# P times V in tiles of 64 rows by 32 columns, each half of a key tile in a PSUM bank of its own

## The chip, the core and the metric

The kernel runs on one core of a Trainium2 chip. The metric is device time of one execution, in microseconds. Three runs of the kernel before took 1716.6 to 1716.94 us, with a median of 1716.67 us.

A core has five engines that run on their own and wait for one another through semaphores. TensorE (PE in the profile) multiplies matrices and writes the products to PSUM, which has eight banks of 128 partitions by 512 float32 values. ScalarE (ACT) and VectorE (DVE) read PSUM, GpSimd (POOL) does not. SyncE (SP) issues nearly all DMAs here.

## The reference

A transformer block with adaptive layer norm, on x of 2048 rows by 512 columns, in float32:

```python
mod = (silu(c) @ w_mod).reshape(1, 6, 1, 512)        # sa, ca, ga, sb, cb, gb
h = layernorm(x) * (1 + ca) + sa
q = (h @ wq) as 32 heads of 16;  k = h @ wk;  v = h @ wv     # one k and one v for all heads
p = softmax(q @ k.T * 16 ** -0.5)
x = x + ga * ((p @ v, heads side by side) @ wo)
h = layernorm(x) * (1 + cb) + sb
x = x + gb * (((h @ w_gate) * (h @ w_up)) @ w_down)          # 512 -> 1792 -> 512
```

The change is in `p @ v`: for each head, 2048 queries by 2048 keys, times 2048 keys by 16 values.

## The kernel before

**Attention.** The 2048 query rows are cut into NB = 4 blocks of 512 and the 32 heads into 8 groups of four: 32 units `u`, each a block of queries and four heads. A unit walks over KT = 16 key tiles of 128 keys; one such step is here called a step, and there are 512 of them. In a step:

- `qk_exp` (line 627) makes, for each of four heads, the scores with keys on partitions and queries on columns (tile `sc`, line 631), and ACT writes their exponential to SBUF as the float32 tile `P` (line 633). Letter e in the order of the step.
- `max_half` and `max_mm` (lines 1050 and 576) make, for the next unit, scores with queries on partitions (tile `mx`, line 581); DVE reduces each to its maximum over 512 keys (line 584). Letter m. The maxima are subtracted inside a later score product, so that the exponential is that of a softmax.
- `pv` (line 637) multiplies V's tile by the four `P` tiles of the key tile one step back. V's tile `vst` has 32 columns: 16 values, and ones that give the sum of the exponentials. Head j's result goes to partitions 32j to 32j + 31 of one PSUM tile, `pvb[u]`, in which all 16 key tiles are summed.

Scores and maxima are float16 products with 48 or 50 rows, split over the two halves of PE's rows by the index `a`: two of them, on different halves, run at the same time. P times V is in float32 and uses all 128 rows and 32 columns for each head.

**Side work.** Between those, PE works on the projections and the gated feed-forward part of the block (tile `side`, line 499; letter x). A group of such products sums in one bank. It too is split into row halves: while a step's e and m use one half, its x use the other, and `half` (line 506) adds a wait for an exponential when the half changes.

**Order.** `attend` (line 1142) writes the order of a pair of steps out by hand. In the early units (projections of q as side work) it is `FEW`, later `MANY`; in `MANY` a step has four e, four m and eight x in the order e m e e m m m e. At the end of a step come the evictions of ended side groups (`finish`) and then `pv` of the step before. A unit's last `pv` therefore runs in the next unit's first step, and `pv_out` of the ended unit is kept in `ends`, which is run in the middle of the step after that:

```python
                if j == len(order) // 2:
                    for f in ends:
                        f()
```

`pv_out` (line 645) copies `pvb[u]` to SBUF (`ev`, ACT, line 648), scaled per partition by `evs`, and five DMAs carry `ev` on to `oc` and `rs`, which `normalise` reads later.

**Banks.** The eight banks are a queue, `pool`. `ps_hold` takes the oldest entry and keeps it until `ps_give` puts it back at the end; `ps_mx`, which `sc` and `mx` use, takes the oldest and puts it back at once, so that its next user waits for whoever still reads it:

```python
        tag, bufs = pool.popleft()
        ...
        pool.append((tag, bufs))
```

`pvb[u]` is held for a whole unit, the side group for its length. A new side group may begin in a step in which the one before it ended; that one's bank comes back at the end of the step.

After the 32 units follow, with nothing of attention beside it, the rest of the side work and the feed-forward part of the last block of queries.

Of the kernel before, what the change touches and what calls it, by code (L numbers as in the profile page):

```python
# [15 lines left out]
AF = mybir.ActivationFunctionType  # L16
OP = mybir.AluOpType
# [8 lines left out]
KT = S // 128  # L26
# [27 lines left out]
def adaln_mqa_glu_kernel(ctx: ExitStack, tc: tile.TileContext, x_in, wq_in, wk_in, wv_in, wo_in,  # L54
                         wg_in, wu_in, wd_in, c_in, wm_in, out):
    nc = tc.nc
# [13 lines left out]
    def ps_hold(name="side", shape=(128, 512)):  # L70

        tag, bufs = pool.popleft()
        t = psum.tile(list(shape), F32, name=name, tag=tag, bufs=bufs)
        held[id(t)] = (t, tag, bufs)
        return t

    def ps_give(t):
        _, tag, bufs = held.pop(id(t))
        pool.append((tag, bufs))
# [53 lines left out]
    vst = consts.tile([128, KT, 32], F32, name="vst")  # L133
    nc.gpsimd.memset(vst, 1.0)
    sst = []
    for i in range(3):
        t = consts.tile([128, 2, BT], F16, name=f"sst{i}")
# [152 lines left out]
    for k in range(KC):  # L290
        for j in range(4):
            nc.tensor.matmul(pmA[32 * j:32 * j + 32, 0:256], silr[:, k, 0:32], wmA[:, k, 256 * j:256 * j + 256],  # L292
                             start=(k == 0), stop=(k == KC - 1))
# [77 lines left out]
    evs = consts.tile([128, 1], F32, name="evs")  # L371
# [249 lines left out]
    pvb = {}  # L621
    ptl = {}
# [13 lines left out]

    def pv(u, kt):
        if kt == 0:
            pvb[u] = ps_hold("pv")
        for j in range(4):  # L640
            p, a = divmod(j, 2)
            nc.tensor.matmul(pvb[u][32 * j:32 * j + 32, :], vst[:, kt, :], ptl[u, kt, p, a],  # L642
                             start=(kt == 0), stop=(kt == KT - 1))

    def pv_out(u):
        b, g = divmod(u, UB)
        ev = work.tile([128, BT], F32, name="ev", tag="ev", bufs=3)
        nc.scalar.activation(ev, pvb[u], AF.Copy, scale=evs)
        ps_give(pvb[u])
        if g % 2 == 0:  # L650
            oc[b, g // 2] = work.tile([128, BT], F32, name="oc", tag="oc", bufs=2)
            rsum[b, g // 2] = dram.tile([8, BT], F32, name=f"rs{b}_{g // 2}")
        h = 4 * (g % 2)
        for j in range(4):
            r = 16 * (h + j)
            nc.sync.dma_start(oc[b, g // 2][r:r + 16, :], ev[32 * j:32 * j + 16, :])
        nc.sync.dma_start(rsum[b, g // 2][h:h + 4, :], ev[16:128:32, :])
# [484 lines left out]
    def attend(u, kt):  # L1142
# [9 lines left out]
        for turn in range(2):  # L1152
# [23 lines left out]
            if v >= 0:  # L1176
                pv(*divmod(v, KT))
                if v % KT == KT - 1:
                    ends.append(lambda: pv_out(u - 1))
# [37 lines left out]
    u = NU - 1  # L1217

    pv(u, KT - 1)
    pv_out(u)  # L1220
    if cur:
        for r in range(2):
# [55 lines left out]
```

## Time and profile before

| what | value |
|---|---|
| median of three runs | 1716.67 us (1716.6 to 1716.94) |
| span of the profiled execution, first to last instruction | 1713.5 us |
| PE busy | 1666.1 us, 97% |
| DVE busy | 1393.1 us, 81% |
| ACT busy | 1218.4 us, 71% |
| POOL busy | 505.1 us, 29% |
| mean granted clock of PE | 0.993 |
| first and last eviction of a unit (start of `ev`) | 140.0 and 1539.5 us |

The page gives no time of the profiled execution beside its span; the runs are some 3 us longer than the span. In the rows of the trace, PE is a matmul and PEld its weight load; a matmul in float32 appears as two records with a weight load each. A row of the timeline has the start in us from the start of the span, the duration, engine, line, operation, the tile written and those read, rows times columns of the array (128*32), the operand's shape and a count if several follow one another. A group of the page has, behind the count, the busy time in us and the mean in ns, and then the idle time of the engine ahead of it and what ended it. A stretch has the busy time of PE, PEld, DVE, ACT and POOL, each with its count.

### The profile page before, as it was taken

The numbers are of one execution on the slowest core, as the hardware profiler recorded it, in microseconds if no ns is written. First come the engines' busy times: TensorE is split into PE (matmuls) and PEld (weight loads), VectorE is DVE, ScalarE is ACT, GpSimd is POOL, SyncE is SP. The second block draws the span as 40 slices with busy tenths as digits, with TensorE's granted clock in tenths as the row PEclk, the third lists the DMA queues.
The fourth block names the chain that finished last, engine by engine and source line by source line (L and its number), as shares of the span: only waits on it lengthen the run. The fifth ranks groups of instructions, "written<-read, shape, count | busy, mean of one in ns | idle before, by whom it ended". The sixth has DMA issues, their size and how long they took to land.

```text
span 1713.5 us, 33210 instructions
## 1 busy us (share of the span) xinstructions
PE 1666.1 (97%) x12671; PEld 538.8 (31%) x12671; DVE 1393.1 (81%) x2364; ACT 1218.4 (71%) x2295; POOL 505.1 (29%) x705
## 2 busy tenths in 40 slices
PE   6799999999999999999999999999999999999999
PEld 3223333222223333333333333333323333334444
DVE  7699999999999999999989999999998999604110
ACT  3668888888888777777787777777777777771010
POOL 5724445535576751110020111101011010103130
PEclk9899999999999999999999999999999999999999
DMA  5212122311222210001100000000100000001000
GB/s 201 85 49 81 60 77 72 93 37 56 82 80 60 65 41 9 16 9 29 34 8 19 13 16 9 16 9 16 31 25 22 12 20 5 8 6 45 14 1 25
DMA packets 48939, 66.64 MB, mean 39 GB/s; under 512 B 15302, under 2 KB 29450, under 8 KB 48780
## 3 DMA queue, kind: packets, MB, share of 16 engines
q1 hardware_dynamic: 47196, 64.33, 12.2%
q8 instruction: 99, 1.62, 0.4%
q14 instruction: 60, 0.49, 0.1%
q10 hardware_dynamic: 1584, 0.20, 0.1%
HBM read 51.12 MB, written 8.92 MB: 35 GB/s over the span
## 4 chain that ended last, share of the span: by engine, by line
PE 86%; DVE 8%; ACT 4%; issue 2%; POOL 1%; ACTq 0%; POOLq 0%
PE side L499 49%; PE pv L642 26%; DVE mpart L584 7%; PE sc L631 5%; PE mx L581 3%; ACT P L633 3%; PE pk L257 1%; PE mx L771 1%; PE pq L352 0%; PE mxt L608 0%; PE sc L247 0%; ACT kwb L250 0%; PE misc L871 0%; PE pv L460 0%; PE misc L292 0%
## 5 line engine op out<-in xcount | busy, mean ns | idle before, releaser
L584 DVE TENSOR_REDUCE mpart<-mx 128x1 f32<-128x512 f32 x2016 | 1267.5, 684 | 107.7 <-PE mx L581 103.1
L633 ACT ACTIVATE P<-sc 128x512 f32<-128x512 f32 x2048 | 1093.7, 599 | 269.1 <-PE sc L631 225.7
L631 PE MATMUL sc<-sst,kst 50*128 50x512 f16 x2048 | 661.4, 379 | 0.8 <-DVE mpart L584 0.6
L581 PE MATMUL mx<-kst,sst 48*128 48x512 f16 x2032 | 617.6, 378 | 8.5 <-DVE mpart L584 5.1
L642 PE MATMUL pv<-P,vst 128*32 128x512 f32 x4096 | 546.2, 605 | 1.2
L499 PE MATMUL side<-h2T,wg 64*128 64x512 f16 (+1 forms) x1152 | 278.3, 378 | 1.5 <-ACT P L633 1.5
L499 PE MATMUL side<-h2T,wu 64*128 64x512 f16 (+1 forms) x1144 | 276.2, 378 | 1.0 <-ACT P L633 1.0
L499 PE MATMUL side<-wd,glu 64*128 64x512 f16 (+1 forms) x1008 | 234.0, 378 | 2.7 <-ACT P L633 2.7
L823 POOL TENSOR_SCALAR glu<-gf 128x512 f16<-128x512 f32 x56 | 34.6, 617 | 654.2 <-DVE gf L822 573.2
L631 PEld LDWEIGHTS <-kst 50*128 50x128 f16 x2048 | 174.5, 94 | 130.8 <-issue 109.7
L581 PEld LDWEIGHTS <-sst 48*128 48x128 f16 x2048 | 182.6, 94 | 64.1 <-issue 42.1
L499 PEld LDWEIGHTS <-wg 64*128 64x128 f16 (+1 forms) x1152 | 99.5, 95 | 209.6 <-ACT P L633 99.3
L499 PEld LDWEIGHTS <-wu 64*128 64x128 f16 (+1 forms) x1144 | 99.0, 95 | 201.7 <-ACT P L633 91.3
L642 PEld LDWEIGHTS pv<-P,vst 128*32 128x32 f32 x4096 | 80.8, 108 | 215.8 <-issue 199.7
L499 PEld LDWEIGHTS <-glu 64*128 64x128 f16 (+1 forms) x1008 | 89.1, 95 | 166.3 <-ACT P L633 66.4
L822 DVE TENSOR_TENSOR gf<-side,g 128x512 f32<-128x512 f32 x56 | 38.4, 685 | 124.0 <-PE side L499 91.0
L816 ACT ACTIVATE g<-side 128x512 f32<-128x512 f32 x56 | 33.3, 595 | 96.8 <-PE side L499 96.8
L499 PE MATMUL side<-h,wq 64*128 64x512 f16 (+1 forms) x372 | 97.0, 379 | 0.0
L499 PE MATMUL side<-wo,och 64*128 64x512 f16 (+1 forms) x336 | 79.3, 378 | 0.4 <-ACT P L633 0.2
L824 POOL TENSOR_TENSOR glu<-gf,glu 128x512 f16<-128x512 f32 x56 | 65.2, 1165 | 4.7
L190 POOL TENSOR_SCALAR rv<-st 128x1 f32<-128x1 f32 (+1 forms) x20 | 4.5, 227 | 162.4 <-DVE st L735 146.7
L909 POOL TENSOR_TENSOR kwb<-kwb,wsl 128x448 f32<-128x448 f32 (+1 forms) x40 | 47.5, 1188 | 3.1
(221 smaller groups left out, 773.7 us busy)
## 6 DMA issues: line engine op xcount, KB each, us to landing
wsl<-in_B_w_gate_dram SPq DMA_DIRECT2D x32, 224.0 KB
wsl<-in_B_w_up_dram SPq DMA_DIRECT2D x32, 224.0 KB
wsl<-in_B_w_down_dram SPq DMA_DIRECT2D x28, 256.0 KB
sst<-qd SPq DMA_DIRECT2D x186, 32.0 KB
qd<-q SPq DMA_DIRECT2D x16, 256.0 KB
oc<-ev SPq DMA_DIRECT2D x128, 32.0 KB
rr<-ri SPq DMA_DIRECT2D x16, 256.0 KB
xl<-in_A_x_dram SPq DMA_DIRECT2D x16, 256.0 KB
```

The costliest lines, as they stand in the source:

```text
L257: nc.tensor.matmul(p, wk3[:, k].rearrange("p a r -> p (a r)"), hf(b, k), start=(k == 0), stop=(k == KC - 1))
L499: return nc.tensor.matmul(self.p, left[64 * r0:64 * r1], right[64 * r0:64 * r1], start=start, stop=self.ended())
L581: nc.tensor.matmul(m, s[64 * a:64 * a + 48, p, t * 128:(t + 1) * 128], keys, start=True, stop=True)
L584: nc.vector.tensor_reduce(part, m, axis=AX.X, op=OP.max)
L631: nc.tensor.matmul(t, kst[64 * a:64 * a + 50, kt * 128:(kt + 1) * 128], s[64 * a:64 * a + 50, p, :], start=True, stop=True)
L633: ex = nc.scalar.activation(ptl[u, kt, p, a], t, AF.Exp)
L642: nc.tensor.matmul(pvb[u][32 * j:32 * j + 32, :], vst[:, kt, :], ptl[u, kt, p, a], start=(kt == 0), stop=(kt == KT - 1))
L816: nc.scalar.activation(st["g", f], p, AF.Copy, scale=2.0 ** -45)
L822: nc.vector.tensor_tensor(gf, p, st["g", f], op=OP.mult)
L823: nc.gpsimd.tensor_scalar(st["glu"][:, 0, f, :], gf, 1.0, 0.0, op0=OP.mult, op1=OP.add)
L824: nc.gpsimd.tensor_tensor(st["glu"][:, 1, f, :], gf, st["glu"][:, 0, f, :], op=OP.subtract)
L909: nc.gpsimd.tensor_tensor(acc, acc, t, op=OP.add)
```

## The change

`pv` now makes eight products instead of four. The 128 keys of a tile are cut into two halves of 64, `r`; each half has its own PSUM tile, so `pvb[u]` is a list of two banks, both held for the unit. At the end, ACT copies the first, scaled, and DVE multiplies the second by the same scale and adds `ev`.

```diff
     def pv(u, kt):
         if kt == 0:
-            pvb[u] = ps_hold("pv")
+            pvb[u] = [ps_hold("pv") for _ in range(2)]
         for j in range(4):
             p, a = divmod(j, 2)
-            nc.tensor.matmul(pvb[u][32 * j:32 * j + 32, :], vst[:, kt, :], ptl[u, kt, p, a],
-                             start=(kt == 0), stop=(kt == KT - 1))
+            for r in range(2):
+                ks = slice(64 * r, 64 * r + 64)
+                nc.tensor.matmul(pvb[u][r][32 * j:32 * j + 32, :], vst[ks, kt, :], ptl[u, kt, p, a][ks],
+                                 start=(kt == 0), stop=(kt == KT - 1))
 
     def pv_out(u):
         b, g = divmod(u, UB)
         ev = work.tile([128, BT], F32, name="ev", tag="ev", bufs=3)
-        nc.scalar.activation(ev, pvb[u], AF.Copy, scale=evs)
-        ps_give(pvb[u])
+        nc.scalar.activation(ev, pvb[u][0], AF.Copy, scale=evs)
+        nc.vector.scalar_tensor_tensor(ev, pvb[u][1], evs[:, 0:1], ev, op0=OP.mult, op1=OP.add)
+        for t in pvb[u]:
+            ps_give(t)
```

## The prediction

> **What bounds the kernel now.** I read the page first: busy times, the chain that ended last, the costliest groups.
>
> ```profile
> span 1713.5 us, 33210 instructions
> PE 1666.1 (97%) x12671; PEld 538.8 (31%) x12671; DVE 1393.1 (81%) x2364; ACT 1218.4 (71%) x2295; POOL 505.1 (29%) x705
> ...
> PE side L499 49%; PE pv L642 26%; DVE mpart L584 7%; PE sc L631 5%; PE mx L581 3%; ACT P L633 3%; PE pk L257 1%; PE mx L771 1%; PE pq L352 0%; PE mxt L608 0%; PE sc L247 0%; ACT kwb L250 0%; PE misc L871 0%; PE pv L460 0%; PE misc L292 0%
> ...
> L642 PE MATMUL pv<-P,vst 128*32 128x512 f32 x4096 | 546.2, 605 | 1.2
> ```
>
> TensorE holds the chain, and P times V (L642) is 26% of it. Its 512 blocks (32 units of 16 key tiles) are never late for their data: 1.2 us of idle time in all. VectorE comes next; the view of busy times by stretch shows how much room it has in the later units:
>
> ```profile
> 900.00:1050.00 150.00, 149.40 (x1245) 46.00 (x1245) 136.69 (x224) 117.51 (x221) 16.73 (x18) 1.00 0.06 15
> ```
>
> Of 150 us, PE is busy for 149.40 and DVE for 136.69. So what lengthens PE's sequence lengthens the kernel; DVE work is free only where nobody waits for it. The timeline around one block:
>
> ```profile
> 802.22 0.38 PE L631 MATMUL sc<-sst,kst 50*128 50x512 f16 x1
> 802.53 0.16 PEld L642 LDWEIGHTS pv<-P,vst 128*32 128x32 f32 x8 [0.43 <-issue]
> 802.53 1.06 PE L642 MATMUL pv<-P,vst 128*32 128x512 f32 x8
> 803.53 0.39 PE L499 MATMUL side<-wd,glu 64*128 64x512 f16 x1
> 803.53 0.39 PE L631 MATMUL sc<-sst,kst 50*128 50x512 f16 x1
> ```
>
> Each float32 matmul is two records, so eight records are four tiles of 128 rows by 32 columns, which run at once. From the block's start to the next matmul pass 1.00 us. Elsewhere in the step, matmuls on the two row halves follow at 0.215 us, the time in which 512 columns stream. The last sc starts at 802.22 and has streamed at 802.44; the block starts 0.09 later. Four passes of 0.213 are 0.85 of its 1.00 us; the rest is some 0.05 of staggered starts and weight loading and some 0.10 at its end.
>
> **The change, part by part.** *The streaming.* Eight tiles of 64 rows hold the same products. If they all run at once, the four passes remain 0.85 us; if the halves of a column strip take turns they are 1.70. The rows at 803.53 show two row halves starting together, and the block shows four column strips together; both at once is not in this trace. I take no change, as both kinds of concurrency are there, and keep turns as a rival.
>
> *More instructions.* Eight weight loads span 0.16 us, each 0.108 by itself, so they start 0.007 us apart. Four more tiles put the last of them 0.027 later in the block: 512 x 0.027 = 14 us on PE's path. Ends: nothing, if the sequencer runs ahead, and 29 us if both passes pay. The Trainium skill, TensorE: Matmul & The Clock Gate, Part 3 ("Measured speedup vs the span model"), gives about 4 ns per further tile; by it this term would be an estimated 8 us.
>
> *One bank fewer.* This is the part that the diff does not name. Eight banks circulate in a queue: a matmul of scores (e, line 631) or of maxima (m, line 581) takes the oldest free one and waits until ACT or DVE has emptied it. The pv tile holds one bank for a whole unit and a side group another, which leaves six. The change holds two for pv, which leaves five. Following the banks along both programs' order: in the 128 steps of the first eight units, 72 go from six uses back to five, 26 from five to four and 24 from seven to six. In the later 384 steps most go from six to five; in 98 a new side group takes its bank in mid-step while the ended one is held until the step ends, and there the second half goes from five to four.
>
> An early step, in order e m e m e m e m; the rows of PE, ACT and DVE:
>
> ```profile
> 236.38 0.39 PE L631 MATMUL sc<-sst,kst 50*128 50x512 f16 x1
> ...
> 237.26 0.38 PE L581 MATMUL mx<-kst,sst 48*128 48x512 f16 x1
> 237.47 0.38 PE L631 MATMUL sc<-sst,kst 50*128 50x512 f16 x1
> 237.58 0.37 PE L581 MATMUL mx<-kst,sst 48*128 48x512 f16 x1
> ...
> 238.88 0.39 PE L631 MATMUL sc<-sst,kst 50*128 50x512 f16 x1
> ...
> 236.80 0.60 ACT L633 ACTIVATE P<-sc 128x512 f32<-128x512 f32 x1 [0.44 <-PE mx L581]
> 237.30 0.59 ACT L633 ACTIVATE P<-sc 128x512 f32<-128x512 f32 x1
> 236.84 0.69 DVE L584 TENSOR_REDUCE mpart<-mx 128x1 f32<-128x512 f32 x1
> ```
>
> Here six banks already bind: the last m (237.58) starts 0.05 after DVE ends the step's first m (236.84 + 0.69 = 237.53), six uses back. So a release takes 0.05. With five, the sixth matmul (237.26) waits for the first e: 236.80 + 0.60 + 0.05 = 237.45. The seventh waits for the first m: 237.58. The last waits for the second e: 237.30 + 0.59 + 0.05 = 237.94, which is 0.36 later than now. The step of 2.50 us becomes 2.86: 72 x 0.36 = 26 us. The 26 steps that drop to four I put at the same 0.36 (9 us), the 24 with a seventh bank to spare at nothing. Together 35 us; ends 13 (half of the waits absorbed) and 44 (all 24 pay too).
>
> A later step, in order e m e e m m m e:
>
> ```profile
> 958.16 0.39 PE L631 MATMUL sc<-sst,kst 50*128 50x512 f16 x1
> ...
> 959.04 0.38 PE L581 MATMUL mx<-kst,sst 48*128 48x512 f16 x1
> 959.26 0.37 PE L581 MATMUL mx<-kst,sst 48*128 48x512 f16 x1
> 959.47 0.37 PE L581 MATMUL mx<-kst,sst 48*128 48x512 f16 x1
> 959.69 0.38 PE L631 MATMUL sc<-sst,kst 50*128 50x512 f16 x1
> ...
> 960.99 0.39 PE L631 MATMUL sc<-sst,kst 50*128 50x512 f16 x1
> ...
> 958.59 0.60 ACT L633 ACTIVATE P<-sc 128x512 f32<-128x512 f32 x1 [0.65 <-PE sc L631]
> 959.10 0.60 ACT L633 ACTIVATE P<-sc 128x512 f32<-128x512 f32 x1
> 959.60 0.59 ACT L633 ACTIVATE P<-sc 128x512 f32<-128x512 f32 x1
> 958.80 0.69 DVE L584 TENSOR_REDUCE mpart<-mx 128x1 f32<-128x512 f32 x1 [0.30 <-PE mx L581]
> ```
>
> With five banks the third of the three m (959.47) waits for the step's first m: 958.80 + 0.69 + 0.05 = 959.54, so 0.07. With four in the second half, 959.04 becomes 958.59 + 0.60 + 0.05 = 959.24; 959.26 becomes 959.54; 959.47 becomes 959.75; and the last e (959.69) waits for the third e: 959.60 + 0.59 + 0.05 = 960.24, 0.55 late. Such a step pays 0.07 today. So 98 x 0.48 + 286 x 0.07 = 67 us; ends 20 (the 98 pay nothing extra) and 91 (the step after each of the 98 loses 0.24 more). The Trainium skill, TensorEngine Tiling (Array Packing), "Gotcha 1: PSUM Pressure", speaks against this change in the same sense: "Row tiling increases PSUM pressure". It gives no price.
>
> *The eviction.* ACT's copy stays as it is, on one half. DVE gets 32 instructions more, priced by its nearest row, L837:
>
> ```profile
> 983.27 0.69 ACT L648 ACTIVATE ev<-pv,evs 128x512 f32<-128x512 f32 x1
> 982.09 0.68 DVE L584 TENSOR_REDUCE mpart<-mx 128x1 f32<-128x512 f32 x1
> 982.09 2.48 DVE L584 TENSOR_REDUCE mpart<-mx 128x1 f32<-128x512 f32 x4
> 983.18 1.07 PE L642 MATMUL pv<-P,vst 128*32 128x512 f32 x8
> 985.17 0.37 PE L631 MATMUL sc<-sst,kst 50*128 50x512 f16 x1
> ...
> L837 DVE SCALAR_TENSOR_TENSOR x<-side,sca,x 128x512 f32<-128x512 f32 x12 | 8.9, 744 | 22.0 <-PE side L499 22.0
> ```
>
> As bare work, 32 x 0.744 = 24 us would fit into DVE's idle time in the later units (13 of 150 us above). Its place does not: by the order of the new program it stands between the first and the second m of the unit's second step, and reads what ACT writes. DVE is through with the first m at 982.77, but ACT ends ev at 983.96. DVE waits till 984.0, adds till 984.75, and the three m behind it end at 985.43, 986.03 and 986.63 (0.60 apart, as 2.48 for four of 0.68 shows). Two things follow on PE. The next unit's pv takes two banks; the second is the one that ACT has just read, so its second row half waits until 984.0 instead of 983.18: 0.8 us. The fourth matmul of the next step takes the bank of the last m: 986.63 + 0.05 against 985.17, 1.5 us late; the 0.8 lies inside it. I take 1.5 at each of the 31 boundaries with a successor, 46 us, and 1 us for the last eviction; ends 25 (0.8 alone) and 62 (DVE's whole delay of 2.0). The five DMAs that carry ev away wait for DVE instead of ACT, about 1 us later; what reads them comes units later. SP's queue behind them carries weights and q with the same distance. The first side matmul after a block waits for the step's last exponential; both move with PE.
>
> *Sum:* 14 + 35 + 67 + 46 + 1 = 163 us. The runs' median, 1716.67, is 3.2 over the profiled span of 1713.5; added to the median, **1880 us**. Low ends: 0 + 13 + 20 + 25 + 1 = 59, 1776. High ends: 29 + 44 + 91 + 62 + 1 = 227, 1944.
>
> **The rivals.** *Faster: the switch of tile shape goes.* Now rows and columns change at the block; afterwards the other matmuls and the block all have 64 rows. If PE then need not drain, up to 0.09 before, 0.10 behind and 0.03 of first weight loading go: 0.22 x 512 = 113 us. It decides only if all other terms stay below 0.22 us per key tile; with the likeliest 163 the kernel would still end at 1767, with the low ends at 1663 (1717 - 113 + 59), which is what I give for it. Against it stands a change of columns alone, where a 128 x 128 transpose follows a block:
>
> ```profile
> 505.73 1.06 PE L642 MATMUL pv<-P,vst 128*32 128x512 f32 x8
> ...
> 506.73 0.44 PE L771 MATMUL mx<-ident,n 128*128 128x128 f32 x2
> ```
>
> It starts 1.00 after the block, as late as where the rows change too. The Trainium skill, TensorEngine Tiling (Array Packing), Key Properties, says that changing the mode drains the engine; by it nothing goes, and the trace agrees.
>
> *The banks do not bind:* evictions shift so that PE rarely waits. Then 14 + 46 + 1 remain, 1778 us. Against it: the early step, where PE waits to the hundredth for the sixth use back.
>
> *The halves take turns:* 0.85 x 512 = 435 us more, 2315.
>
> **How the numbers follow.** The sum as worked out (1800 to 1944) has 0.66; banks that hardly bind 0.15; the switch gone and the kernel faster 0.11; turns 0.06; no change 0.02. The range of 1760 to 1945 takes in the first two and the bounds, and leaves out the other 0.19. Over 0.2% (3.4 us, about what a measurement of this kernel can tell): faster 0.11, within 0.02, slower 0.87.
>
> **What the profile after would show.** Right: step times of about 2.9 in the later units with every third near 3.4, early ones near 2.9; the idle time ahead of lines 631 and 581 grown from 9 us to over 80, ended by DVE and ACT; the new DVE instruction waiting for ACT about 1.2 us each time. The block should be about 1.03 us from its start to the next matmul. Wrong: a block well under 1.00 (switch gone), near 1.85 (turns), or steps still at 2.84 (banks free).

## The result and the profile after

The changed kernel takes 1881.78 us (median of four runs, 1881.02 to 1882.09) against 1716.63 for the kernel before (median of four): a ratio of 1.0967, with a 95% interval of 1.0951 to 1.0983. The page of its profiled execution, cut to the busy times, the chain that ended last and the groups that the prediction speaks of:

```profile
span 1879.8 us, 41463 instructions
PE 1804.8 (96%) x16767; PEld 549.6 (29%) x16767; DVE 1426.5 (76%) x2396; ACT 1228.4 (65%) x2295; POOL 506.7 (27%) x705
...
PE side L499 32%; PE pv L644 26%; ACT P L633 13%; PE sc L631 8%; PE mx L581 8%; DVE mpart L584 2%; DVE ev L651 1%; ACT ev L650 1%; PE pk L257 1%; DMA wmA<-in_w_mod_dram 1%; PE mx L775 0%; PE pq L352 0%; PE sc L247 0%; PE mxt L608 0%; ACT kwb L250 0%
...
L581 PE MATMUL mx<-kst,sst 48*128 48x512 f16 x2032 | 656.4, 377 | 28.7 <-ACT P L633 12.1
L631 PE MATMUL sc<-sst,kst 50*128 50x512 f16 x2048 | 665.4, 378 | 13.1 <-DVE mpart L584 4.3
L644 PE MATMUL pv<-P,vst 64*32 64x512 f32 x8192 | 573.3, 601 | 2.5 <-ACT ev L650 1.4
...
L651 DVE SCALAR_TENSOR_TENSOR ev<-pv,evs,ev 128x512 f32<-128x512 f32 x32 | 24.0, 751 | 45.8 <-ACT ev L650 45.8
```

The span grew by 166.3 us. It lies 1.8 us below the time of the same run, 1881.64; in the runs of the kernel before whose spans are on record it is 1.8 to 2.1, so the 3 us named ahead compare different executions. The busy share of PE says nothing of it, 96% after 97%. The chain does: the exponentials (ACT P) now hold 13% of it, some 240 us, where they held 3%, some 50 us. P times V still has its 26% and no data to wait for, 2.5 us of idle time in all. The same stretch of the busy times as before, in the later units:

```profile
900.00:1050.00 150.00, 147.79 (x1495) 44.14 (x1490) 127.52 (x211) 108.76 (x201) 17.98 (x43) 1.00 0.08 22
```

DVE and ACT did less in it, 127.52 us against 136.69 and 108.76 against 117.51. PE too stands idle for longer, 2.21 us against 0.60. So the program is held by waits and not by work that one of the three gained.

The trace shows where. The starts of the 512 blocks of P times V give 511 step times for each kernel, which can be taken from each other one by one. They sum to 166.3 us; ahead of the first block and behind the last one nothing over 0.3 us changed. (The 511th, in which the last two blocks follow one another, is 0.88 us in both and not in the table.)

| steps | count | mean before | mean after | sum of the differences |
|---|---|---|---|---|
| first eight units | 113 | 2.56 | 3.00 | 49.9 |
| their two steps at each change of unit | 15 | 2.65 | 3.06 | 6.1 |
| later, a side group begins in mid-step | 86 | 2.95 | 3.41 | 39.6 |
| later, no new side group | 249 | 2.87 | 3.01 | 35.0 |
| later, two steps at each change of unit | 47 | 3.03 | 3.79 | 35.7 |

Every kind of step pays. First an early step in order e m e m e m e m, in the timeline of the kernel after (PE, then ACT):

```profile
246.37 0.39 PE L631 MATMUL sc<-sst,kst 50*128 50x512 f16 x1
...
247.50 0.37 PE L581 MATMUL mx<-kst,sst 48*128 48x512 f16 x1
...
247.99 0.37 PE L581 MATMUL mx<-kst,sst 48*128 48x512 f16 x1
248.29 1.09 PE L644 MATMUL pv<-P,vst 64*32 64x512 f32 x16
...
246.86 0.60 ACT L633 ACTIVATE P<-sc 128x512 f32<-128x512 f32 x1 [0.74 <-PE mx L581]
247.35 0.59 ACT L633 ACTIVATE P<-sc 128x512 f32<-128x512 f32 x1
```

The sixth matmul (247.50) starts when the first exponential has ended and a release has passed, 246.86 + 0.60 + 0.05 = 247.51. The eighth (247.99) does so behind the second one, 247.35 + 0.59 + 0.05 = 247.99. Both are five uses back, where it was six before. From the first to the last matmul it is 1.62 us, where the step shown of before took 1.20.

A later step in which a side group begins, in order e m e e m m m e (PE, then ACT and DVE):

```profile
1064.26 0.39 PE L631 MATMUL sc<-sst,kst 50*128 50x512 f16 x1
...
1065.33 0.37 PE L581 MATMUL mx<-kst,sst 48*128 48x512 f16 x1
...
1065.67 0.37 PE L581 MATMUL mx<-kst,sst 48*128 48x512 f16 x1
...
1066.34 0.37 PE L631 MATMUL sc<-sst,kst 50*128 50x512 f16 x1
1066.64 1.09 PE L644 MATMUL pv<-P,vst 64*32 64x512 f32 x16
1067.66 0.39 PE L499 MATMUL side<-h2T,wu 64*128 64x512 f16 x1
...
1064.68 0.60 ACT L633 ACTIVATE P<-sc 128x512 f32<-128x512 f32 x1 [0.75 <-PE sc L631]
...
1065.69 0.59 ACT L633 ACTIVATE P<-sc 128x512 f32<-128x512 f32 x1
...
1064.93 0.69 DVE L584 TENSOR_REDUCE mpart<-mx 128x1 f32<-128x512 f32 x1 [0.45 <-PE mx L581]
```

Here only four banks circulate in the second half. The fifth matmul waits for the first exponential (1064.68 + 0.60 + 0.05 = 1065.33), the sixth for the first maximum (1064.93 + 0.69 + 0.05 = 1065.67), and the last e for the third exponential (1065.69 + 0.59 + 0.05 = 1066.33). It starts 2.08 us behind the first one, against 1.53 in the step shown of before. The block itself takes 1.02 from its start to the next matmul.

A change of unit (ACT's copy, the new addition, the next unit's first block, and the step behind it):

```profile
1097.90 0.69 ACT L650 ACTIVATE ev<-pv,evs 128x512 f32<-128x512 f32 x1
...
1098.63 0.75 DVE L651 SCALAR_TENSOR_TENSOR ev<-pv,evs,ev 128x512 f32<-128x512 f32 x1 [1.28 <-ACT ev L650]
...
1100.49 0.68 DVE L584 TENSOR_REDUCE mpart<-mx 128x1 f32<-128x512 f32 x1
...
1098.07 1.67 PE L644 MATMUL pv<-P,vst 64*32 64x512 f32 x16
...
1099.67 0.39 PE L631 MATMUL sc<-sst,kst 50*128 50x512 f16 x1
...
1101.22 0.37 PE L631 MATMUL sc<-sst,kst 50*128 50x512 f16 x1 [0.21 <-DVE mpart L584]
...
1102.39 1.09 PE L644 MATMUL pv<-P,vst 64*32 64x512 f32 x16
...
1104.09 0.37 PE L631 MATMUL sc<-sst,kst 50*128 50x512 f16 x1
```

DVE stands idle for 1.28 us, then adds, and is late with three maxima. The last of them ends at 1101.17, and the fourth matmul of the next step (1101.22) starts 0.05 later. That is 3.15 us behind its block's start, where the fourth matmul of the following step (1104.09) has 1.70. The block before it is stretched to 1.60 us, since its second bank is the one that ACT reads until 1098.59. From block to block it is 4.32 us, 1.31 more than in a step without a change of unit.

### The profile page after: what moved, and what is told of

Its sections match the earlier page's. It is cut to its first block, busy times and chain, and to the rows that moved or that the text cites. A ratio compares the mean times of both kernels' runs of the same rounds, so it can differ in the third digit from the quotient of the medians.

```text
span 1879.8 us, 41463 instructions
## 1 busy us (share of the span) xinstructions
PE 1804.8 (96%) x16767; PEld 549.6 (29%) x16767; DVE 1426.5 (76%) x2396; ACT 1228.4 (65%) x2295; POOL 506.7 (27%) x705
## 4 chain that ended last, share of the span: by engine, by line
PE 78%; ACT 14%; DVE 4%; issue 2%; DMA 1%; POOL 1%; ACTq 0%; SPq 0%; DVEq 0%; POOLq 0%
PE side L499 32%; PE pv L644 26%; ACT P L633 13%; PE sc L631 8%; PE mx L581 8%; DVE mpart L584 2%; DVE ev L651 1%; ACT ev L650 1%; PE pk L257 1%; DMA wmA<-in_w_mod_dram 1%; PE mx L775 0%; PE pq L352 0%; PE sc L247 0%; PE mxt L608 0%; ACT kwb L250 0%
## 5 line engine op out<-in xcount | busy, mean ns | idle before, releaser
L581 PE MATMUL mx<-kst,sst 48*128 48x512 f16 x2032 | 656.4, 377 | 28.7 <-ACT P L633 12.1
L631 PE MATMUL sc<-sst,kst 50*128 50x512 f16 x2048 | 665.4, 378 | 13.1 <-DVE mpart L584 4.3
L644 PE MATMUL pv<-P,vst 64*32 64x512 f32 x8192 | 573.3, 601 | 2.5 <-ACT ev L650 1.4
L499 PE MATMUL side<-h2T,wg 64*128 64x512 f16 (+1 forms) x1152 | 285.0, 378 | 0.2 <-ACT P L633 0.2
L499 PE MATMUL side<-h2T,wu 64*128 64x512 f16 (+1 forms) x1144 | 281.9, 378 | 0.0
L644 PEld LDWEIGHTS pv<-P,vst 64*32 64x32 f32 x8192 | 96.7, 104 | 285.2 <-issue 256.8
L499 PE MATMUL side<-h,wq 64*128 64x512 f16 (+1 forms) x372 | 112.6, 384 | 0.0
L651 DVE SCALAR_TENSOR_TENSOR ev<-pv,evs,ev 128x512 f32<-128x512 f32 x32 | 24.0, 751 | 45.8 <-ACT ev L650 45.8
```

Of the source, the lines that this page charges most:

```text
L499: return nc.tensor.matmul(self.p, left[64 * r0:64 * r1], right[64 * r0:64 * r1], start=start, stop=self.ended())
L581: nc.tensor.matmul(m, s[64 * a:64 * a + 48, p, t * 128:(t + 1) * 128], keys, start=True, stop=True)
L631: nc.tensor.matmul(t, kst[64 * a:64 * a + 50, kt * 128:(kt + 1) * 128], s[64 * a:64 * a + 50, p, :], start=True, stop=True)
L644: nc.tensor.matmul(pvb[u][r][32 * j:32 * j + 32, :], vst[ks, kt, :], ptl[u, kt, p, a][ks], start=(kt == 0), stop=(kt == KT - 1))
L651: nc.vector.scalar_tensor_tensor(ev, pvb[u][1], evs[:, 0:1], ev, op0=OP.mult, op1=OP.add)
```

## The experiments

The theory was the prediction's: most of the time is lost because one bank less circulates, some because of DVE's addition, little because of the eight small tiles. The rivals were that the tile shape itself makes PE slower or faster, and that the addition, which is the only new wait in the diff, carries the larger part.

**Two banks without small tiles.** The even key tiles are summed in one bank and the odd ones in the other, in tiles of 128 rows, with the same eviction:

```diff
-            nc.tensor.matmul(pvb[u][32 * j:32 * j + 32, :], vst[:, kt, :], ptl[u, kt, p, a],
-                             start=(kt == 0), stop=(kt == KT - 1))
+            nc.tensor.matmul(pvb[u][kt % 2][32 * j:32 * j + 32, :], vst[:, kt, :], ptl[u, kt, p, a],
+                             start=(kt < 2), stop=(kt >= KT - 2))
```

> Two banks per unit, filled by even and odd key tiles, added at the eviction as in the changed kernel; the tiles stay 128 rows by 32 columns. The result is the reference's. Theory (the held bank and the place of the addition cost the time, the tile shape only 0.018 us per block, the difference of the blocks in the two traces): 1881.8 - 512 x 0.018 = 1872 us, range 1866 to 1878. Rival (the small tiles themselves cost it, by their loads, switches or writes): below 1760 us.

It takes 1869.42 us (1868.48 to 1871.48), a ratio of 1.0901 (1.0883 to 1.092). The tile shape is worth the 12.4 us between this and the kernel after. In the traces it is 13.1 us (spans 1866.7 and 1879.8); 12.4 of them lie between the first block and the last, spread over the steps at 0.01 to 0.05 each. The remaining 153 us need no small tile.

**The bank alone.** The kernel before, with one entry of the queue put aside for as long as a unit's bank is held:

```diff
+    spare = {}
...
         if kt == 0:
             pvb[u] = ps_hold("pv")
+            spare[u] = [pool.popleft() for _ in range(1)]
...
         ps_give(pvb[u])
+        pool.extend(spare[u])
```

> The kernel before, with one bank more taken out of the queue for the length of each unit and not used. Theory: the waits for banks alone. From the step times of the two traces: early steps +0.42 us each (54 us over 128), later ones +0.12 for 249 and +0.44 for 86 plus some 7 at boundaries (76 us): 1717 + 130 = 1847 us, range 1835 to 1860. Rival (tile shape): 1717 us within 5. Rival (the addition): below 1730 us.

1841.95 us in one run, with a span of 1840.0: 126.5 us over the span before, without a second eviction and with the old tiles. The line of the maxima, in the groups of this kernel:

```profile
L581 PE MATMUL mx<-kst,sst 48*128 48x512 f16 x2032 | 656.8, 376 | 30.4 <-ACT P L634 13.5 <-DVE sst L263 1.6 <-DVE mpart L584 0.7
```

Busy 656.8 us and idle 30.4, ended by the exponentials (here line 634), as in the kernel after (656.4 and 28.7). By steps: 50.1 us in the first eight units, 37.8 in the later steps in which a side group begins (0.44 each), 29.9 in the 249 others (0.12 each), 9.4 at the later changes of unit. That is 127.1; outside the blocks this execution is 0.7 us shorter than that of before. The step from here to the kernel above, 26.7 us in the spans, is the addition: 25.8 of them lie in the 47 later steps at a change of unit, 1.1 in the 15 early ones, and the other 448 steps agree to 0.2 us in all. So the 166.3 us are 126.5 for the bank, 26.7 for the eviction and 13.1 for the tiles by the spans, and 127.1, 26.7 and 12.4 by the steps.

The early steps hold something that the prediction did not see. Where q's projections have run out of side work, two e and two m follow one another in pairs. The last row of the following fence is ACT's first exponential of the step, the others are PE's; the kernel before:

```profile
339.23 0.39 PE L631 MATMUL sc<-sst,kst 50*128 50x512 f16 x2
339.45 0.38 PE L581 MATMUL mx<-kst,sst 48*128 48x512 f16 x2
339.68 0.38 PE L631 MATMUL sc<-sst,kst 50*128 50x512 f16 x2
339.98 0.70 PE L581 MATMUL mx<-kst,sst 48*128 48x512 f16 x2
...
339.65 0.60 ACT L633 ACTIVATE P<-sc 128x512 f32<-128x512 f32 x1 [0.31 <-PE sc L631]
```

and such a step of the kernel after:

```profile
378.22 0.39 PE L631 MATMUL sc<-sst,kst 50*128 50x512 f16 x2
378.45 0.38 PE L581 MATMUL mx<-kst,sst 48*128 48x512 f16 x2
378.67 0.38 PE L631 MATMUL sc<-sst,kst 50*128 50x512 f16 x2
379.35 0.86 PE L581 MATMUL mx<-kst,sst 48*128 48x512 f16 x2 [0.30 <-ACT P L633]
...
378.70 0.60 ACT L633 ACTIVATE P<-sc 128x512 f32<-128x512 f32 x1 [0.88 <-PE sc L631]
```

With seven banks only the eighth matmul waits for the first exponential (339.65 + 0.60 + 0.05 = 340.30, inside the last row). With six the seventh does, 378.70 + 0.60 + 0.05 = 379.35, and the eighth waits for the second one. From the first matmul to the start of the last pair it is 1.13 us instead of 0.75. Of the 24 steps that the prediction had put at nothing, the 23 that can be matched pay 11.8 us in this experiment, 0.51 each; the 70 that go from six to five pay 26.7 (0.38 each), the 22 that go from five to four 7.8 (0.35 each). The same order comes back later: of the 249 later steps without a new side group, 16 have no side work at all. They pay 7.1 of the 29.9 us, 0.45 each; the other 233 pay 0.10 each.

**The small tiles alone.** Tiles of 64 rows, on the first 64 keys of each key tile alone, so four of them and one bank; the copy adds 1 in place of the second half, and the eviction stays on ACT:

```diff
-            nc.tensor.matmul(pvb[u][32 * j:32 * j + 32, :], vst[:, kt, :], ptl[u, kt, p, a],
+            ks = slice(0, 64)
+            nc.tensor.matmul(pvb[u][32 * j:32 * j + 32, :], vst[ks, kt, :], ptl[u, kt, p, a][ks],
...
-        nc.scalar.activation(ev, pvb[u], AF.Copy, scale=evs)
+        nc.scalar.activation(ev, pvb[u], AF.Identity, bias=1.0, scale=evs)
```

> The kernel before with P times V in tiles of 64 rows by 32 columns, but only the first 64 keys of each key tile: four products per block, one bank, no addition; half of the keys are left out, and 1 is added to the evicted tile so that no sum is zero. Theory (streaming is by columns, and the change of columns alone still drains PE): blocks of 1.00 us, 1717 us, range 1711 to 1722. Rival (with 64 rows throughout PE need not drain): down to 1717 - 512 x 0.19 = 1620 us. Rival (small tiles cost the time): over 1740 us.

The median is 1771.49 us, 1737.63 to 1786.09; PE's mean granted clock was 0.944 to 0.979 in its four runs, the longer the run the lower, against 0.993 to 0.996 in the runs of the kernel before. So the time was missed by 54 us, and the shape has to be read from stretches at full clock. Three stretches of this kernel, in the view of busy times (the last but two numbers of a row is the granted clock):

```profile
130.00:146.00 16.00, 16.00 (x78) 3.41 (x76) 8.73 (x14) 7.23 (x13) 0.00 (x0) 0.50 0.06 12
425.00:490.00 65.00, 65.00 (x289) 11.01 (x289) 43.96 (x74) 37.15 (x73) 31.14 (x38) 0.50 0.16 47
900.00:1000.00 100.00, 98.73 (x806) 30.79 (x808) 89.29 (x149) 78.57 (x147) 12.89 (x32) 1.00 0.06 16
```

and a block of the last one, in the timeline:

```profile
975.54 0.38 PE L631 MATMUL sc<-sst,kst 50*128 50x512 f16 x1
975.85 1.06 PE L643 MATMUL pv<-P,vst 64*32 64x512 f32 x8
976.85 0.39 PE L631 MATMUL sc<-sst,kst 50*128 50x512 f16 x1
```

At full clock nothing moved: of the 53.6 us by which the span of this run is longer, 52.6 lie in 35 steps in or beside the stretches at 0.50, and the other 476 steps differ by 1.1 us in all. The block starts 0.31 us after the last e, as before (802.22 to 802.53), though both now have 64 rows, and it takes 1.00. The switch from 128 columns to 32 and back costs the same with and without a change of rows; the rival in which it goes is out. So what the kernel after pays for its tiles comes with there being eight of them, on both row halves. The Trainium skill, TensorEngine Tiling (Array Packing), Key Properties, has it that changing the mode drains the engine; by these rows a change of columns alone is enough for the same gap.

**The addition alone.** The kernel before, with DVE adding the same bank once more behind ACT's copy, so that values and sums of the exponentials are both doubled and their quotient stays:

```diff
         nc.scalar.activation(ev, pvb[u], AF.Copy, scale=evs)
+        nc.vector.scalar_tensor_tensor(ev, pvb[u], evs[:, 0:1], ev, op0=OP.mult, op1=OP.add)
```

> The kernel before with the addition on VectorE at its place in the eviction, reading the one bank a second time, so that P times V comes out doubled: the eviction's part alone, with six banks in the queue. Theory: DVE is 2.0 us late behind the addition; with six banks the fourth matmul of the next step takes the bank of the last but one m and is 0.9 us late; 24 later boundaries x 0.9 = 22 us, nothing in the early units: 1739 us, range 1728 to 1750. Rival (the 24 us of work find room in VectorE's idle time): 1717 within 4. Rival (the addition is the main cost): over 1780 us.

1749.46 us in one run, 33.5 over the kernel before on that chip (1715.96): just inside the range, and half as much again as the 22 us that were expected. The later steps at a change of unit pay 29.7 us, the early ones, put at nothing, 4.5. With one bank less the same addition cost 26.7, with 1.1 in the early units. The two costs do not add up fully; in the early units, where the banks already hold PE back, the addition is nearly free.

**Two banks put aside.** The `range(1)` of the second experiment becomes `range(2)`.

> The kernel before with two banks more held idle for each unit: the dose doubled, four left in the queue and three behind a new side group. Theory, by the same walk as in the prediction: an early step of 2.50 us becomes 3.10 (0.60 for the last m, 128 steps, 77 us), a later plain one pays 0.55 (298 x 0.55 = 164 us), one with a new side group 1.0 (86 us): 1716 + 327 = 2043 us, range 1990 to 2110. Rival (the price per bank is a constant, 126 us as for the first): 1968 us.

2021.65 us in one run; the second bank costs 180 us after 126 for the first. The chain of waits of this kernel:

```profile
ACT P L634 28%; PE pv L644 25%; PE side L499 16%; PE sc L632 12%; PE mx L581 5%; DVE mpart L584 2%; ACT ev L650 1%; PE pk L257 1%; DMA wmA<-in_w_mod_dram 1%; PE mx L774 0%; PE pq L352 0%; ACT hf L781 0%; PE sc L247 0%; PE mxt L608 0%; ACT kwb L250 0%
```

The exponentials now hold more of it than any line of PE. The plain later steps, which paid 0.12 each for the first bank, pay 0.53 for both, and those in which a side group begins 0.87 (0.44). A constant price per bank is out.

**The addition moved to the end of the step.** The kernel after, with ACT's copy in its old place, and DVE's addition and all that follows it behind the step's last maximum:

```diff
+    late = []
...
         nc.scalar.activation(ev, pvb[u][0], AF.Copy, scale=evs)
+        late.append(lambda: pv_add(u, ev))
+
+    def pv_add(u, ev):
+        b, g = divmod(u, UB)
         nc.vector.scalar_tensor_tensor(ev, pvb[u][1], evs[:, 0:1], ev, op0=OP.mult, op1=OP.add)
...
             assert not sync["due"]
+            for f in late:
+                f()
+            late.clear()
             for g in ended:
                 g.finish()
...
     pv_out(u)
+    late.pop()()
```

> The changed kernel with VectorE's addition, and what follows it, moved to the end of the same step: behind the three m, ahead of the next unit's first P times V. The same instructions, another place. Theory (27 of the 166 us are the place): ACT has written ev by the time DVE comes to the addition, so DVE does not wait; what is left is some 0.3 us at each of 24 later boundaries, 1882 - 20 = 1862 us, range 1855 to 1869. Rival (it is the work of the addition, or the second bank that it holds): 1882 us within 4, or more as the banks come free later.

1860.38 us (1859.86 to 1860.58), a ratio to the kernel before of 1.0844 (1.0826 to 1.0862). The later steps at a change of unit get 23.4 us back, the rest of the steps lose 3.6. The new group, and one of its instructions in the timeline:

```profile
L656 DVE SCALAR_TENSOR_TENSOR ev<-pv,evs,ev 128x512 f32<-128x512 f32 x32 | 23.8, 743 | 14.9 <-ACT ev L651 14.9
```

```profile
1090.26 0.74 DVE L656 SCALAR_TENSOR_TENSOR ev<-pv,evs,ev 128x512 f32<-128x512 f32 x1
```

The addition takes about as long as before, 0.743 us after 0.751. DVE stands idle ahead of only the last two of the 32, for 3.6 and 11.3 us as in the kernel after; ahead of the other 30, where it stood idle for 30.9 us, it no longer waits at all. It was the waiting ahead of the maxima that cost PE its time, and hardly the 24 us of DVE work.

**The ended side group given up sooner.** In the later steps in which a side group begins, the bank of the ended one is held to the end of the step. Its eviction is issued where the group ends, in the kernel after and in the kernel before:

```diff
             if self.ended():
-                ended.append(self)
+                self.finish()
```

The kernel after with this edit:

> The changed kernel with the eviction of an ended side group issued where the group ends, not at the end of the step, so that its bank comes back in mid-step. Followed along the program, the steps with four uses back fall from 202 to 128 of 384, and in these the last e no longer waits. Theory: such a step loses 0.28 instead of 0.55 us: 98 x 0.27 = 26 us less, 1856 us, range 1845 to 1870. Rival (the eviction, now queued ahead of the exponentials and maxima on ACT and DVE, costs as much as the bank gives): 1882 us within 5.

1879.34 us (1878.84 to 1879.88), a ratio to the kernel before of 1.0954 (1.0938 to 1.0971). The forecast of a gain of 26 us fell, and the rival holds: the gain is 2.4 us. Up to 1.3 of it may be the chip, on which the kernel before too took 1715.33 us instead of 1716.63. ACT and PE in such a step:

```profile
1161.26 0.59 ACT L820 ACTIVATE g<-side 128x512 f32<-128x512 f32 x1
...
1161.91 0.37 PE L631 MATMUL sc<-sst,kst 50*128 50x512 f16 x1
```

The last e no longer waits for the third exponential. It takes the bank of the ended group, whose eviction now stands ahead of that exponential on ACT and ends at 1161.85; the e starts 0.06 later. That is 2.09 us behind the step's first matmul (at 1159.82), where it was 2.08 in the step shown of the kernel after: a bank has come back, but only through the same queue of ACT. In the mean these steps went from 3.41 to 3.37 us.

The kernel before with this edit:

> The kernel before with the same earlier eviction of side groups. With six banks the last e of such a step does not wait, so theory gives little: 1714 us, range 1704 to 1722. If the second side bank were what costs the kernel before its 2.91 us steps, 98 x 0.07 = 7 us would go, 1709 us. Rival (the earlier eviction blocks ACT): over 1722 us.

1724.21 us (1723.32 to 1724.84), a ratio of 1.005 (1.0035 to 1.0065): slower by 8.9 us, 8.0 in the spans. The expected range ended at 1722, so this was missed too, and the rival holds: the early eviction delays the exponentials behind it. In 37 steps the first matmul behind the block waits longer than in the kernel before, 8.1 us in all (in eight others it waits 3.6 us less). In most of the 37 it starts 1.16 us behind the block's start instead of 1.00: the side product there waits for the step's last exponential, which now comes later on ACT. No version with two banks for P times V beat the kernel before.

## Why the prediction came out right

The forecast was 1880, the runs gave 1881.78. It lies inside the range of 1760 to 1945. The mechanisms were the ones named, but the agreement to 2 us is partly luck: two terms were too small and two too large.

| term | predicted | measured | from |
|---|---|---|---|
| eight tiles instead of four | 14 | 13 | kernel after less the one with two banks and old tiles |
| one bank fewer, first eight units | 35 | 50 | kernel before with one bank put aside |
| one bank fewer, later units | 67 | 77 | the same, 37.8 + 29.9 + 9.4 |
| eviction | 47 | 27 | two banks and old tiles less one bank put aside |
| sum | 163 | 167 (166.3 in the spans) | |

*The streaming and the instructions.* Eight tiles of 64 rows run at once, as taken: the block takes 1.02 us, not near 1.85. The 0.027 per block became 0.01 to 0.05 by kind of step, and the term stands. The 8 us worked out from the Trainium skill, TensorE: Matmul & The Clock Gate, Part 3, were too few.

*One bank fewer, early.* The rule that a matmul waits until the bank is free that was used six, now five, uses ago held to the hundredth of a microsecond in the steps shown. The step priced wrongly is "the 24 with a seventh bank to spare at nothing": they run in pairs, as the one shown does, e e m m e e m m, and with six banks the seventh matmul meets the first exponential. They pay 0.51 each, 11.8 us. The 70 others that can be matched pay 0.38 in the mean, where 0.36 was forecast. The typical one pays 0.42, since its first exponential starts 0.49 us behind its matmul instead of 0.42; why it does was not followed up.

*One bank fewer, later.* The last e of a step in which a side group begins is 0.55 late, as worked out (2.08 less 1.53), and these steps pay 0.44 to 0.46 where 0.48 was taken. The others were put at 0.07 and pay 0.12; with 249 of them that is 12 us, which is more than the 10 missing. About half of it is the 16 without side work, which the prediction overlooked here as in the early units (0.45 each); the rest is 0.10 instead of 0.07 in the other 233. The Trainium skill, TensorEngine Tiling (Array Packing), "Gotcha 1: PSUM Pressure", named the direction; the price here is 126.5 us of a span of 1713.5.

*The eviction.* DVE waits for ACT 1.28 us in the median, as in the step shown, forecast 1.2; the mean is 1.1 (45.8 us less the 11.3 of the longest, over 31), as the early ones wait less. The fourth matmul of the next step is late as described, by 1.45 (3.15 less 1.70). What failed is the factor, "1.5 at each of the 31 boundaries". The 1.45 is not the price of the step. From block to block 1.31 of it are left in the step shown, and against the kernel with one bank put aside, whose steps pay their waits for banks there too, it is 25.8 us at the 24 later changes of unit, 1.1 each. At the seven early ones it is 0.16 each (1.1 us).

*What the profile after would show.* Later steps near 2.9 with others near 3.4, early ones near 2.9, and a block of 1.03: the trace has 3.01, 3.41, 3.00 in the mean, and 1.02. Those near 3.4 are one in four, not "every third". The idle time ahead of lines 631 and 581 was to pass 80 us and reached 41.8 (13.1 + 28.7). The waits are there, but do not show as idle time. A matmul's record lasts 0.38 us where the next one may start 0.215 behind it, so a wait of up to 0.16 is covered by the record in front, and one behind a side matmul on the other half likewise. The same 2032 records of line 581 with a mean of 377 ns cover 656.4 us instead of 617.6 because they overlap less. The chain, with its 13% for the exponentials, was the view to name.

*The rivals.* That the switch of tile shape goes was refuted by the tiles of 64 rows alone; that the banks do not bind, by the bank put aside; that the halves take turns, by the block of 1.02 us.

## What to carry to other kernels

Before a tile is given a second PSUM bank, count how many banks are left in circulation, and walk through each kind of step, asking whose reader the n-th matmul now waits for. Do it for every order of the work, the one with banks to spare too, since there the order can move the wait onto the first reader. Where an engine that empties banks gets an instruction that waits for another engine, put it behind the readers that somebody waits for: that gave back 23 of 27 us at the changes of unit here, and 21 us of the whole, with the same work.

## What was not expected of the hardware

With half of P's rows left out, PE's granted clock fell to 0.50 in stretches in which PE was never idle: 65.00 of 65 us busy between 425 and 490 us of the span, with 289 matmul records, where the kernel before has this:

```profile
425.00:490.00 65.00, 63.44 (x481) 17.72 (x477) 63.60 (x110) 52.46 (x100) 41.59 (x71) 1.00 0.28 81
```

It kept its clock. Idle time ahead of the fall does not tell the two apart: between 350 and 400 us, before this stretch began at about 411, PE was busy for 47.52 of 50 us with half of the rows, and for 46.81 in the kernel before. The Trainium skill, TensorE: Matmul & The Clock Gate, Part 1, knows 4/8 as the state of an idle PE and 8/8 as that of a busy one; the value agrees with the 0.50 seen, the condition does not, as far as busy time shows it. Whether the smaller share of the array in use brought it about is open: no run varied that by itself, and the kernel after, which uses all rows, ran at 0.995.
